# Attention with a mixture of experts: expert 0's first 384 rows are turned by TensorE instead of DMA transposes, and the planner's ranks are set anew

## The chip, the cores and the metric

One core of one Trainium2 chip. The metric is the device time of one execution in microseconds; shown is the median of several runs.

## What is computed

Local attention with a linear position bias over 8 batches, 8 heads, 576 positions and head size 64, then a layer of 8 experts in which each of the 4608 rows goes to its two best by noisy logits:

```python
mask = (rel >= 0) & (rel < 128)
scores = np.where(mask, q @ k.T / 8 - slope * abs(rel), -1e9)
x = (softmax(scores) @ v).reshape(4608, 512)
noisy = x @ w_gate + log1p(exp(x @ w_noise)) * noise
top2 = the two largest of the 8 noisy logits of a row, weighted by softmax
for e in range(8):
    h = np.maximum(x[mask] @ w1[e], 0.0)           # 512 -> 1024
    out[mask] += weight[mask] * (h @ w2[e])        # 1024 -> 512
```

## The kernel before

**Stages.** The attention goes through 32 pairs of heads: scores into banks of the accumulator memory (L557, L568), bias and row maximum on VectorE (L572), exponentials on ScalarE (L596), transposes of the weights by TensorE (L610, L614), copies out (L306 or L310, the two branches of one helper), masks on GpSimd (L633, L634), the product with the values (L647, L656). Per batch the result `xu` is turned into rows (L816), scaled and stored to DRAM (`xs`); a small product gives the gate logits (L849), and `route` makes from them, on all engines, the list of rows of each expert (`slots`, L1039).

**Expert 0 starts early.** Its first 1024 rows are three blocks, `first[0]` to `first[2]`: 384 rows known after batch 4, 384 after batch 6, 256 after batch 7 (`FIRST`, L28). The rest of expert 0 (192 rows) and the other experts' wide blocks of 512 rows, which save multiplications by sums of quarters (L1521), come after the attention.

**A block's way.** `first_ids` loads the row numbers; `tokens` (L1364) gathers 128 rows at a time by an indirect DMA from GpSimd's queue (L1369) into one of three buffers; `turn_tokens` (L1470) calls `fit` (L1444): ScalarE sums squares (L1463), VectorE makes powers of two (L536 to L1455), ScalarE or VectorE writes the high fp16 part (L1465), VectorE the low part (L1466). The two parts are then turned by two DMA transposes issued on SP's queue, in `across` (L1484, L1487), into `xhe` and `xle`, features on partitions. The parts' buffers (`partr`, three pairs) come free only when both have landed (L1480, L1481), and the block is ready when all its tiles are.

**The products.** Each matrix is split in an fp16 high and low part. A first product of a step (`mm1`, L1492) is 12 instructions (4 chunks of features by 3 combinations of parts), `middle` makes the two parts of the hidden rows, and a second product (`mm2`, L1641) adds 3 instructions for each 128 rows; a block has 8 steps of 128 hidden columns. The weights of a step are loaded through small buffers (`raw`, L1353) and split (L1358, L1359). Banks: until the attention's scores are all done, the scores hold four; then three go to the ring `yb` of the second product and one to the ring `hbr` of the first; the attention's other banks join `hbr` when it ends (`banks`, L1778).

**The order.** All instructions are issued in a fixed order for each engine, written out when the program is built. A small planner (`Order`, L110) runs the strands as coroutines with estimated durations and takes, on each engine, the ready operation of the lowest rank; `either` lets ScalarE or VectorE take a copy, whichever comes first. The ranks are sums of a place in the work and tuned constants (`GATE`, `ROUTE`, `FINE`, `STAGE` and so on, L44 to L70). An engine runs its list strictly in that order. In `route`, batches in `QUICK` do seven small elementwise operations (L910 to L912 and L980 to L983) on VectorE, the others on GpSimd.

```python
ring_ = partr if blk in first else tpr
yield either(0.61, 0.6, FINE[108] + rank, LATE[6], lambda e: copy(e, hi[0:r], xg[0:r, 0:DM], scale=up_))
for src, to in ((hi, blk.xh), (lo, blk.xl)):
    spawn(across(src[0:r], to[:, :, cs], rank, landed))
```

Of the kernel before, what the change touches and what calls it, by code (L numbers as in the profile page):

```python
# [9 lines left out]
F16 = mybir.dt.float16  # L10
# [4 lines left out]
OP = mybir.AluOpType  # L15
# [25 lines left out]
WIDE, HALF = 512, 256  # L41
REST = CAP - 2 * WIDE
BLOCKS = tuple(((FROWS, c - FROWS),) if z < NF else ((0, WIDE), (WIDE, WIDE), (2 * WIDE, c - 2 * WIDE)) for z, c in enumerate(CAPS))
ZERO, EMPTY = -382.3, -19  # L44
LOAD = 2072.8
VALUES = -625.0
GATE = (3971.6, 412.2, 111.3, 51.8, 791.7, 789.6, 2069.7, 1294.1)
ROUTE = (335.8, 1160.5, 1403.3, 167.8, 383.8, 836.8, 2175.7, 1956.5)
SCATTER = (-4836.6, 2231.2, -4386.9, -2680.6, 1116.4, -5442.0, 1062.3, 4922.0)
FFN0, FFN1 = -16.7, 677.3  # L50
WEIGHTS = (4140.0, 489.6)
TOKENS = -1020.1
FINE = (-127.3, 1947.0, 7173.5, 490.3, -2780.2, 5954.0, 637.9, -361.7, -649.3, -210.9, -151.3, -905.5, -37.6, -1880.9, 2484.8, 98.4, -658.3, 297.3, -173.4, 348.7, 1057.7, 92.6, 695.5, -338.5, 101.0, 1053.3, -1871.9, 74.4, -170.0, -319.0, 74.0, -244.9, -243.9, 2608.1, 50.9, -18.3, 1061.6, 362.2, -2980.7, 6.3, -2268.2, -402.2, 2094.6, -340.9, 153.2, 699.4, 5518.7, -1010.4, -3064.5, 46.0, -483.1, -595.9, 36.8, -151.2, -384.2, -24.7, 993.6, 28.1, -542.3, -548.0, -4777.1, -2371.4, -0.2, -3348.7, -476.4, -550.6, -2493.0, -1125.3, -1392.5, -827.5, -398.3, -1585.4, -5878.8, 2224.6, 938.3, 3072.0, 4384.7, -465.1, 1415.1, 15.0, -1827.3, -4500.0, 1363.2, -386.3, 3864.4, 4822.7, 160.2, 214.5, 46.3, -2198.5, 357.9, 461.9, -49.1, 263.5, -4035.4, 145.2, -2994.6, 13.2, -185.1, -304.8, -311.6, -535.4, -382.4, 47.0, -739.9, -1144.9, 1496.2, 256.4, 138.3, 640.0, 1746.2, 227.4, 1127.5, -4604.4, -1176.0, -5921.3, -64.4, -1108.1, -841.1, -109.7, -946.5, -120.2, -801.1, -639.7, 262.5, -2170.2, -215.4, 592.8, 436.1, 508.3, 558.9, 299.5, 3603.8, 608.9, 607.1, -370.9, -4584.9, -169.7, -701.5, -4103.9, 1089.3, 315.2, -1365.3, -2191.1, 3868.8, -73.9, -531.1, 7.5, 949.6, 1615.7, -226.8, 149.6)
STAGE = (1189.0, -287.5, 1897.0, -16.5, 17.2, 982.3, 1489.3, 922.7)
MIDDLE = 1219.1
RESULT = 718.4
SIZES = (1329.5, 5070.7, 6603.9)
SOON = -530.0
TIGHT = (1, 5, 7)
QUICK = (5,)  # L60
LATE = (1469.7, 178.7, 538.9, 1188.3, 2256.5, -632.2, -940.3, -218.8, 1749.2, -1178.9, -1654.2, -1776.8, -2806.5, -183.7, -5853.3)
LAG = 0.2
ADD, TWS = 0.34, 5
BEHIND = 176.2
TURN, MARGIN, LATE_BY = (0.3, 0.3), 1.0, 1.0
TURNED = 7e4
SLACK = 0.8
PACE, READ_BY, AHEAD = 1.1, 2.0, 268.0
HELD = 3
SWITCH, NEAR = 0.093, 447.5  # L70
TOP, SOFT, SPLIT = (1.25, 1.25, 0.76), (1.56, 1.56, 0.8), (0.85, 1.35, 0.85)
SP_COST = 0.45
DMA_RATE = 300e3
# [36 lines left out]
class Order:  # L110
# [16 lines left out]
    def spawn(self, strand):  # L127
        self.alive += 1
        self.at(self.now, lambda: self.advance(strand, None))
# [31 lines left out]
    def put(self, ring, tile_):  # L161
        ring.free.append(tile_)
        self.serve(ring)
# [105 lines left out]
def attention_moe(ctx: ExitStack, tc: tile.TileContext, qk_, v, w_gate, w_noise, noise, w1, w2,  # L269
                  out, xs, slots, eye):  # L270
    nc = tc.nc
    ctx.enter_context(tc.manual_schedule())
    main = ExitStack()
    const = ctx.enter_context(tc.tile_pool(name="const", bufs=1))
# [9 lines left out]
    spawn, put, mark = order.spawn, order.put, order.set  # L284
# [4 lines left out]
    def pe(us, rank, emit, join=True, mode="full"):  # L289
        return Op((("PE", us, rank),), emit, join, mode)  # L290
# [4 lines left out]
    def dve(us, rank, emit, join=True, port=False):  # L295
        return Op((("DVE", us, rank),), emit, join, None, port)
# [4 lines left out]
    def either(a, b, rank, late, emit):  # L301
        return Op((("ACT", a, rank), ("DVE", b, rank + late)), emit)

    def copy(e, o, i, **kw):
        if e == "ACT":
            nc.scalar.activation(o, i, AF.Copy, **kw)  # L306
        elif kw:
            nc.vector.tensor_scalar(o, i, kw["scale"], None, op0=OP.mult)  # L308
        else:
            nc.vector.tensor_copy(o, i)  # L310
# [20 lines left out]
    n = len(units)  # L331
# [9 lines left out]
    rel, rel4 = scratch[0][:, 0:W], scratch[0][:, W:2 * W]  # L341
    rel5 = scratch[1][:, 0:BW]
    ident = const.tile([128, 128], F32, name="ident")
    bias = const.tile([128, H, BW], BF16, name="bias")
    bias4 = const.tile([128, NP, W], BF16, name="bias4")
    own_key = const.tile([128, 64], F32, name="own_key")
# [37 lines left out]
    def masks():  # L384
        def folded():
            usual = rel5[:, 64:192]
            nc.vector.tensor_scalar(own_key, rel4[:, 0:64], 0.0, None, op0=OP.is_ge)
            nc.vector.tensor_scalar(usual, rel4, 0.0, float(W), op0=OP.is_lt, op1=OP.mult)
            nc.vector.tensor_add(usual, usual, rel4)
            nc.vector.tensor_copy(rel5[:, 0:64], usual[:, 64:128])  # L390

        def of_first():
            first_ = rel5[:, 192:320]
            nc.vector.tensor_copy(first_[64:128], rel5[64:128, 64:192])
            nc.vector.tensor_scalar(first_[0:64], rel4[0:64], 0.0, 2.0 ** 40, op0=OP.is_lt, op1=OP.mult)
            nc.vector.tensor_add(first_[0:64], first_[0:64], rel4[0:64])

        def bias_of(e, h):
            copy(e, bias[:, h], rel5, scale=slope(h))
            part = slice(h // 2 % 2 * 64, h // 2 % 2 * 64 + 64)  # L400
            copy(e, bias4[part, h // 4 * 2 + h % 2], rel5[part, 64:192], scale=slope(h))

        yield dve(0.14, FINE[0] + -40, lambda: nc.vector.tensor_scalar(ident, rel, 0.0, None, op0=OP.is_equal))
        yield dve(0.14, FINE[1] + -40, lambda: nc.vector.tensor_scalar(before, rel, 0.0, None, op0=OP.is_lt))
        yield dve(0.7, FINE[2] + -40, folded)
        yield dve(0.7, FINE[3] + -40, of_first)
        for g in range(NP):
            for h in (2 * g, 2 * g + 1):
                yield either(0.65, 0.45, FINE[4] + -20 + 5 * g, LATE[9], lambda e, h=h: bias_of(e, h))
            mark(biased[g])  # L410
# [70 lines left out]
    hbr, yb = Ring([]), Ring([])  # L481
# [7 lines left out]
    def loads():  # L489

        for k in range(PAIRS):
            rank = 5 * k - LOAD
            t = qks[k] = yield (qkr, FINE[5] + rank)
            left[k] = len(GROUPS)
# [6 lines left out]
    def all_values():  # L501
        for y in range(2 * B):
            rank = 10 * y - VALUES
            if y == 0:
# [167 lines left out]
    def unit(u):  # L672
        k, gr = units[u]
        blocks = GROUPS[gr]
        t = k * NQ + blocks[0]
        r0, r1, r2, r3, r4, r5, r6, r7 = (t + z for z in STAGE)
        last = gr == 2
# [97 lines left out]
    def rows(b, last, t):  # L775
# [3 lines left out]
        nr, nz = 64 if last else 128, len(blocks)  # L779
        rank = t - GATE[b]  # L780

# [25 lines left out]
    def row_major(b, i, xu, den, t, done):  # L807

        rank = t - GATE[b]
        rows = 64 if i == 4 else 128  # L810
# [27 lines left out]
    def gate(b, blocks, xu, den, t, done):  # L838


        rank = t - GATE[b]
        nz, i = len(blocks), blocks[0]
# [52 lines left out]
    def route(b):  # L895
# [4 lines left out]
        ln, pl = lp[:, 0], lp[:, 1]  # L900
        rank = 20 * b - ROUTE[b]
        V = nc.vector
# [138 lines left out]

        rank = 20 * b + SCATTER[b]
        yield (listing, FINE[63] + rank)
# [106 lines left out]
    first = [Block(0, s0, c, cut * S, own) for (s0, c, cut), own in zip(FIRST, rings1)]  # L1150
# [9 lines left out]
    def weight_rank(e, f):  # L1160

        return 1000 + step_of(e) + f - 4 if e else WEIGHTS[0] + WEIGHTS[1] * f

# [119 lines left out]
    def early_sizes():  # L1283

        yield biased[NP - 1]
        for e in range(EARLY):
# [7 lines left out]
            yield done  # L1294
            yield from powers_of_weights(e, SIZES[e])

# [173 lines left out]
    def turn_tokens(blk, j, r, xg, rank):  # L1470
        yield max(order.now + 3.4, order.transfer(order.now, 2048.0 * r))
        hi, lo, ring_, got = yield from fit(blk, j, r, xg, rank)
        put(xgr if blk in first else xpr, xg)
        mark(blk.weighed)
        yield order.now + MARGIN
        landed = Event(2)
        cs = slice(j * 128, j * 128 + r)
        for src, to in ((hi, blk.xh), (lo, blk.xl)):
            spawn(across(src[0:r], to[:, :, cs], rank, landed))
        yield landed  # L1480
        put(ring_, got)  # L1481
        mark(blk.ready)

    def across(src, to, rank, landed, size=TURNED):  # L1484

# [288 lines left out]
    def first_tokens():  # L1774
        for z, blk in enumerate(first):
            yield from tokens(blk, ranks1[8 * z] - TOKENS)

# [206 lines left out]
    with ExitStack() as ob:  # L1984
# [3 lines left out]
        with tc.For_i(0, reach, 1) as j:  # L1988
            e = nc.values_load(tab[:, 0, bass.ds(j, 1)], engines=[mybir.EngineType.SP], min_val=0, max_val=E - 1)
            r = nc.values_load(tab[:, 1, bass.ds(j, 1)], engines=[mybir.EngineType.SP], min_val=0,  # L1990
                               max_val=(E * EROWS - 128) // LESS)
# [13 lines left out]
            t = op.tile([128, 4, 128], F32, name="ot")  # L2005
# [18 lines left out]
            o = ow.tile([128, DM], F32, name="oo")  # L2024
# [44 lines left out]
```

## Time and profile before

| | |
|---|---|
| median of 3 runs | 979.95 us (979.79 to 980.11) |
| the profiled execution's own time | 978.81 us |
| its span, first to last instruction | 977.1 us |
| mean granted TensorE clock | 0.99 |
| TensorE busy | 943.9 us (97%) |
| VectorE busy | 802.2 us (82%) |
| ScalarE busy | 583.7 us (60%) |
| GpSimd busy | 365.0 us (37%) |
| DMA transposes of `xhe` and `xle` over the whole run | 22 and 22 |

Times in the trace count from the first instruction. PE is TensorE's matrix products, PEld its weight loads, DVE VectorE, ACT ScalarE, POOL GpSimd, SPq the DMA queue of SyncE. The granted clock is the share of TensorE's full speed: 1.00 is 2.4 GHz, 0.50 is 1.2 GHz, and a value between is a mean over a stretch. The drawn length of one product includes its latency, so that products in a row overlap: their rate is seen from their starts. The share of busy time is a mean over stages with different limits: up to about 220 us the attention, from there the experts.

### The profile page before, as it was taken

Reading aid. Unit: us, or ns where it says so; the run is one execution under the profiler, and the core shown is the slowest. Engines: PE = TensorE matmul, PEld = TensorE weight load, DVE = VectorE, ACT = ScalarE, POOL = GpSimd, SP = SyncE. Lnnn points to the kernel's source line nnn. Section 1 sums busy time; section 2 is a strip of 40 time slices with the busy share of each in tenths; the row PEclk is TensorE's granted clock in tenths of the full one; section 3 lists DMA queues with packets and bytes.
Section 4 is the critical chain, followed back from the end, with each engine's and each line's share of the span. In section 5 each row is a group of like instructions: output and inputs, shape, how many; then the busy total and the mean of one; then the engine's idle time right before and its main releaser. Section 6 shows DMA issues by size and latency. Waiting matters only on the chain. (4 is left out here: it accounts for less than half of the span.)

```text
span 977.1 us, 25069 instructions
## 1 busy us (share of the span) xinstructions
PE 943.9 (97%) x8896; PEld 663.7 (68%) x8896; DVE 802.2 (82%) x2768; ACT 583.7 (60%) x1554; POOL 365.0 (37%) x577
## 2 busy tenths in 40 slices
PE   7999999869999999999999999999999999999996
PEld 5777777645557857786677768675867586667753
DVE  8989999979568979997979898978878798979520
ACT  8999988754455745666545556654656365546312
POOL 4467676774424033321342323233322412241113
PEclk9999999989999999999999999999999999999998
DMA  9688998777799797997978889958996969876123
GB/s 330 230 301 273 285 339 271 225 186 148 176 244 180 221 209 148 182 238 201 172 142 202 199 145 210 246 133 161 164 269 140 230 157 235 133 178 127 21 33 52
DMA packets 237151, 188.87 MB, mean 193 GB/s; under 512 B 147872, under 2 KB 191168, under 8 KB 237024
## 3 DMA queue, kind: packets, MB, share of 16 engines
q1 hardware_dynamic: 219680, 148.31, 59.5%
q0 software_dynamic: 17344, 38.94, 21.4%
q8 instruction: 70, 1.15, 0.5%
q14 instruction: 57, 0.47, 0.2%
HBM read 116.24 MB, written 40.71 MB: 161 GB/s over the span
## 5 line engine op out<-in xcount | busy, mean ns | idle before, releaser
L1756 POOL DMA_INDIRECT out_dram<-yo,ix x69 | 116.4, 1687 | 248.2 <-ACT yo L306 142.9
L1652 PEld LDWEIGHTS <-hh 128*128 128x128 f16 x896 | 87.5, 98 | 86.3
L1620 ACT ACTIVATE hh<-bank 128x256 f16<-128x256 f32 (+8 forms) x131 | 45.7, 353 | 114.8 <-PE bank L1521 63.8
L1369 POOL DMA_INDIRECT xp<-xs_dram,ix x35 | 39.8, 1136 | 190.9 <-DVE ix L1116 98.3
L1652 PE MATMUL bank<-w2ha,hh 128*128 128x512 f16 x288 | 109.2, 379 | 0.0
L1652 PE MATMUL bank<-w2la,hh 128*128 128x512 f16 x288 | 109.2, 379 | 0.0
L1652 PE MATMUL bank<-w2ha,hl 128*128 128x512 f16 x288 | 109.2, 379 | 0.0
L596 ACT ACTIVATE p<-p,nm 128x128 f32<-128x128 f32 x256 | 99.1, 396 | 4.2 <-DVE nm L572 4.1
L1521 PEld LDWEIGHTS <-wth 128*128 128x128 f16 x896 | 87.3, 98 | 15.5
L1620 ACT ACTIVATE hh<-c 128x256 f16<-128x256 f32 (+1 forms) x100 | 50.8, 525 | 58.6 <-DVE c L1590 58.2
L306 ACT ACTIVATE yo<-bank,gw 128x512 f32<-128x512 f32 (+6 forms) x61 | 41.7, 686 | 70.3 <-PE bank L1652 45.3
L1652 PEld LDWEIGHTS <-hl 128*128 128x128 f16 x448 | 43.9, 98 | 52.8
L572 DVE CUSTOM_DVE_ANT_0 p<-bank,bias 128x128 f32<-128x128 f32 x288 | 67.0, 285 | 0.3
L306 ACT ACTIVATE c<-bank 128x256 f32<-128x256 f32 x98 | 36.8, 380 | 48.9 <-PE bank L1521 46.8
L557 PE MATMUL bank<-qk 64*64 64x192 f32 (+2 forms) x1152 | 59.2, 325 | 6.8 <-DMA qk<-in_qk_dram 4.6
L1581 DVE TENSOR_TENSOR c<-bank,c 128x512 f32<-128x512 f32 x56 | 38.5, 687 | 30.9 <-PE bank L1521 30.0
L647 PE MATMUL bank<-pT,vraw 128*64 128x128 f32 (+1 forms) x640 | 58.8, 332 | 3.7 <-POOL pT L634 2.5
L1521 PE MATMUL bank<-xhe,wth 128*128 128x256 f16 x224 | 61.1, 273 | 0.0
L1521 PE MATMUL bank<-xlw,wth 128*128 128x256 f16 x224 | 61.1, 273 | 0.0
L1521 PE MATMUL bank<-xhw,wtl 128*128 128x256 f16 x224 | 61.1, 273 | 0.0
L1521 PE MATMUL bank<-xhw,wth 128*128 128x256 f16 x224 | 61.1, 273 | 0.0
L1521 PE MATMUL bank<-xhe,wtl 128*128 128x256 f16 x224 | 61.1, 273 | 0.0
(338 smaller groups left out, 3079.5 us busy)
## 6 DMA issues: line engine op xcount, KB each, us to landing
raw<-in_w_dram SPq DMA_DIRECT2D x144, 256.0 KB, 4.6
mraw<-in_w_dram SPq DMA_DIRECT2D x56, 512.0 KB, 6.1
qk<-in_qk_dram SPq DMA_DIRECT2D x32, 576.0 KB, 5.6
vraw<-in_v_dram SPq DMA_DIRECT2D x16, 640.0 KB, 6.7
out_dram<-xg SPq DMA_DIRECT2D x20, 512.0 KB, 6.4
xs_dram<-x SPq DMA_DIRECT2D x72, 128.0 KB, 4.2
out_dram<-yo,ix POOLq DMA_INDIRECT x69, 5.7
xs_dram<-xg SPq DMA_DIRECT2D x2, 512.0 KB
```

What stands on the lines that cost most here:

```text
L306: nc.scalar.activation(o, i, AF.Copy, **kw)
L557: nc.tensor.matmul(s[h][r * 64:r * 64 + 64, o:o + n_ * 64], qk[half, m * 64:m * 64 + 64], blocks_of(qk[half, QW:QW + S], first_, step, n_) ...
L572: nc.vector.tensor_tensor_reduce(out=o, in0=i, in1=by, scale=-0.125, scalar=3.0e38, op0=OP.add, op1=OP.min, accum_out=m)
L596: nc.scalar.activation(pv, pv, AF.Exp, bias=nm[:, z, h:h + 1], scale=-1.0, accum_out=den[:, i, 2 * g + h:2 * g + h + 1])
L647: nc.tensor.matmul(y, t[:, kb, hh:hh + D], w, start=m == 0, stop=m == len(lst) - 1)
L1369: nc.gpsimd.indirect_dma_start(out=o, out_offset=None, in_=xs[0:blk.rows], in_offset=bass.IndirectOffsetOnAxis(ap=blk.at[0:r, j:j + 1], ax ...
L1521: nc.tensor.matmul(t, wp[:, at + kc], xp[:, 2 * o + kc], start=not add and kc + z == 0, stop=kc + z == 3, skip_group_check=add)
L1581: yield dve(0.6, FINE[125] + rank - MIDDLE, lambda: nc.vector.tensor_tensor(both, y, both, op=OP.add))
L1620: nc.scalar.activation(o, i, AF.Relu)
L1652: nc.tensor.matmul(blk.y[j], h[:, cs], wp, start=a == 0 and z + m == 0, stop=a == 3 and z + m == 3)
L1756: ins = nc.gpsimd.indirect_dma_start(out=out, out_offset=bass.IndirectOffsetOnAxis(ap=blk.ix[0:r, j:j + 1], axis=0), in_=t[0:r], in_offset ...
```

## The change

For the first block alone, the two parts of each 128 rows are no longer sent through DMA transposes. A bank of the second product's ring is taken, seen as fp16 (2 parts x 4 chunks x 128 columns), eight TensorE transposes per 128 rows write into it (24 in all), and two copies of 128x512 by ScalarE or VectorE bring the turned parts to `xhe` and `xle` (six in all). The parts' buffers come free after the copies. An fp16 identity is made at the start. Batch 6 joins `QUICK`. All of the planner's rank constants have new values, so that the order may differ anywhere; the durations that the planner assumes are the old ones.

```diff
-QUICK = (5,)
+QUICK = (5, 6)
-STAGE = (1189.0, -287.5, 1897.0, -16.5, 17.2, 982.3, 1489.3, 922.7)
+STAGE = (1235.4, -299.1, 2758.5, 66.9, 68.8, 3072.9, 2531.1, 1334.1)
-TOKENS = -1020.1
+TOKENS = -1033.3
-FFN0, FFN1 = -16.7, 677.3
+FFN0, FFN1 = -16.4, 567.8
...
+    ident16 = const.tile([128, 128], F16, name="ident16")
...
+        yield dve(0.14, FINE[152] + -40, lambda: nc.vector.tensor_scalar(ident16, rel, 0.0, None, op0=OP.is_equal))
...
         mark(blk.weighed)
+        if blk is first[0]:
+            yield from turned_here(blk, j, r, hi, lo, rank)
+            put(ring_, got)
+            return
         yield order.now + MARGIN
...
+    def turned_here(blk, j, r, hi, lo, rank):
+
+        a = yield (yb, FINE[153] + rank)
+        t = a.bitcast(F16).rearrange("p (z c n) -> p z c n", z=2, c=4)
+
+        def turn():
+            for z, src in enumerate((hi, lo)):
+                for c in range(4):
+                    nc.tensor.transpose(t[:, z, c, 0:r], src[0:r, c * 128:c * 128 + 128], ident16[0:r, 0:r])
+
+        yield pe(0.45, FINE[154] + rank, turn)
+        cs = slice(j * 128, j * 128 + r)
+        done = Event(2)
+        for z, to in enumerate((blk.xh, blk.xl)):
+            spawn(out_of_turn(to[:, :, cs], t[:, z, :, 0:r], rank, done))
+        yield done
+        put(yb, a)
+        mark(blk.ready)
+
+    def out_of_turn(o, i, rank, done):
+        yield either(0.57, 0.6, FINE[155] + rank, LATE[6], lambda e: copy(e, o, i))
+        mark(done)
```

## Rows read from the trace of the kernel before

**Rows 1.** Busy time by stretches: PE, PEld, DVE, ACT, POOL; clock, DMA share, GB/s.

```profile
20.00:160.00 140.00, 136.55 (x2277) 100.87 (x2277) 133.37 (x807) 131.73 (x560) 89.45 (x209) 1.00 0.88 290
160.00:200.00 40.00, 35.46 (x515) 25.75 (x512) 38.43 (x211) 30.01 (x119) 26.98 (x51) 0.96 0.77 229
200.00:208.00 8.00, 5.43 (x82) 3.93 (x79) 7.73 (x24) 5.19 (x17) 5.59 (x7) 1.00 0.71 191
208.00:222.30 14.30, 8.87 (x70) 5.16 (x69) 7.64 (x39) 3.94 (x11) 9.94 (x20) 0.64 0.73 206
222.30:240.00 17.70, 17.70 (x126) 10.93 (x122) 16.89 (x76) 9.15 (x23) 10.23 (x25) 1.00 0.71 121
240.00:961.20 721.20, 719.50 (x5579) 502.54 (x5578) 581.08 (x1508) 384.58 (x755) 210.53 (x224) 1.00 0.82 174
```

**Rows 2.** TensorE's waits from 160 to 225 us: total, times, longest.

```profile
PE bank L647 <- POOL pT L634: 2.5, 2, 1.8
PE bank L610 <- ACT gt L306: 1.8, 1, 1.8
PE bank L656 <- POOL pTl L634: 1.8, 1, 1.8
```

**Rows 3.** The timeline of TensorE: start, length; in brackets idle before it.

```profile
217.12 1.97 PE L816 MATMUL bank<-ident,xu 128*128 128x128 f32 x8
...
222.28 0.32 PE L1495 MATMUL bank<-xhe,w1ha 128*128 128x384 f16 x1
...
251.03 0.33 PE L1495 MATMUL bank<-xhe,w1ha 128*128 128x384 f16 x1
...
281.52 0.27 PE L1495 MATMUL bank<-xhe,w1ha 128*128 128x256 f16 x1
...
319.60 0.27 PE L1521 MATMUL bank<-xhw,w1hb 128*128 128x256 f16 x1
```

**Rows 4.** The timeline of ScalarE (first line) and VectorE: the first block's fit.

```profile
193.49 0.19 ACT L1463 ACTIVATION_READ_ACCUMULATOR th<-xg 128x1 f32 x1
...
198.35 0.28 DVE L572 CUSTOM_DVE_ANT_0 p<-bank,bias 128x128 f32<-128x128 f32 x1
...
198.56 0.15 DVE L536 TENSOR_SCALAR fit<-fit 128x1 int32<-128x1 int32 x1
...
205.15 0.73 DVE L1466 SCALAR_TENSOR_TENSOR th<-xg,fit,th 128x512 f16<-128x512 f32 x1
```

**Rows 5.** The timeline of SP's DMA queue: start, time the issue held it.

```profile
204.89 1.34 SPq L1487 DMA_TRANSPOSE xhe<-th  x1
...
213.04 1.22 SPq L1487 DMA_TRANSPOSE xle<-th  x1
...
214.31 3.17 SPq L1353 DMA_DIRECT2D raw<-in_w_dram  x6
...
236.45 1.22 SPq L1487 DMA_TRANSPOSE xle<-th  x1
...
263.59 1.29 SPq L1487 DMA_TRANSPOSE xle<-th  x1
...
301.81 1.52 SPq L1487 DMA_TRANSPOSE xlw<-th  x1
```

**Rows 6.** The tile xhe from 200 to 300 us: its transposes' landing.

```profile
DMA to landing us min/median/max: 7.9/7.9/7.9
```

**Rows 7.** The timeline of TensorE: runs of small instructions.

```profile
160.87 0.58 PE L963 MATMUL bank<-hot,hot 128*80 128x64 f16 x10
...
189.65 1.09 PE L816 MATMUL bank<-ident,xu 128*128 128x128 f32 x8
```

**Rows 8.** Groups by line and shape: count | busy us, mean ns | idle.

```profile
L816 PE MATMUL bank<-ident,xu 128*128 128x128 f32 x96 | 15.1, 293 | 0.1
...
L306 ACT ACTIVATE xu<-bank 128x512 f32<-128x512 f32 x16 | 9.5, 593 | 7.9 <-PE bank L647 7.9
```

**Rows 9.** The timeline of VectorE: a wait for batch 6's GpSimd operations.

```profile
217.32 0.44 DVE L918 MAX8 tp<-l 128x8 f32<-128x8 f32 x5 [3.92 <-POOL l L983]
```

More of the change, by code (lines that the diff above doesn't have):

```diff
@@ L43 @@
 BLOCKS = tuple(((FROWS, c - FROWS),) if z < NF else ((0, WIDE), (WIDE, WIDE), (2 * WIDE, c - 2 * WIDE)) for z, c in enumerate(CAPS))
[L44 to L49, printed above, removed]
-FFN0, FFN1 = -16.7, 677.3
-WEIGHTS = (4140.0, 489.6)
-TOKENS = -1020.1
-FINE = (-127.3, 1947.0, 7173.5, 490.3, -2780.2, 5954.0, 637.9, -361.7, -649.3, -210.9, -151.3, -905.5, -37.6, -1880.9, 2484.8, 98.4, -658.3, 297.3, -173.4, 348.7, 1057.7, 92.6, 695.5, -338.5, 101.0, 1053.3, -1871.9, 74.4, -170.0, -319.0, 74.0, -244.9, -243.9, 2608.1, 50.9, -18.3, 1061.6, 362.2, -2980.7, 6.3, -2268.2, -402.2, 2094.6, -340.9, 153.2, 699.4, 5518.7, -1010.4, -3064.5, 46.0, -483.1, -595.9, 36.8, -151.2, -384.2, -24.7, 993.6, 28.1, -542.3, -548.0, -4777.1, -2371.4, -0.2, -3348.7, -476.4, -550.6, -2493.0, -1125.3, -1392.5, -827.5, -398.3, -1585.4, -5878.8, 2224.6, 938.3, 3072.0, 4384.7, -465.1, 1415.1, 15.0, -1827.3, -4500.0, 1363.2, -386.3, 3864.4, 4822.7, 160.2, 214.5, 46.3, -2198.5, 357.9, 461.9, -49.1, 263.5, -4035.4, 145.2, -2994.6, 13.2, -185.1, -304.8, -311.6, -535.4, -382.4, 47.0, -739.9, -1144.9, 1496.2, 256.4, 138.3, 640.0, 1746.2, 227.4, 1127.5, -4604.4, -1176.0, -5921.3, -64.4, -1108.1, -841.1, -109.7, -946.5, -120.2, -801.1, -639.7, 262.5, -2170.2, -215.4, 592.8, 436.1, 508.3, 558.9, 299.5, 3603.8, 608.9, 607.1, -370.9, -4584.9, -169.7, -701.5, -4103.9, 1089.3, 315.2, -1365.3, -2191.1, 3868.8, -73.9, -531.1, 7.5, 949.6, 1615.7, -226.8, 149.6)
@@ L54 @@
-STAGE = (1189.0, -287.5, 1897.0, -16.5, 17.2, 982.3, 1489.3, 922.7)
[L55 to L58, printed above, removed]
+ZERO, EMPTY = -1717.1, -19
+LOAD = 5805.0
+VALUES = -1156.0
+GATE = (3497.0, 552.0, -72.8, 105.8, 607.5, 848.8, 1802.4, 1248.6)
+ROUTE = (1229.1, 1099.1, 2641.1, 425.7, 379.3, 1128.2, 1752.3, 1867.2)
+SCATTER = (-5849.4, 2075.8, -4417.3, -3415.7, -149.1, -5144.8, -2198.5, 8121.8)
+FFN0, FFN1 = -16.4, 567.8
+WEIGHTS = (3494.5, 1230.6)
+TOKENS = -1033.3
@@ new lines @@
+FINE = (1659.9, 1149.0, 3054.3, 1123.7, -4771.6, 10025.6, 1545.6, 142.5, -669.6, -1475.9, 609.1, -725.9, -161.1, -1462.1, 1924.9, 33.9, -1495.9, -1094.0, 2143.2, 1838.5, 668.2, 875.6, 721.0, -907.2, -172.0, 1806.9, -198.1, -221.1, -2297.2, -1373.6, 142.0, 554.3, 1143.0, 2468.9, -276.6, -6.4, 109.9, 407.0, -3316.7, 0.7, -1337.7, -94.3, 1709.1, -374.0, -319.4, 23.2, 6303.5, -1535.1, -3283.8, 332.0, -814.2, -1427.5, 126.9, -99.6, -299.7, -2392.7, -279.2, -17.7, 11.2, -976.5, -7262.7, -2312.9, -12.1, -4434.6, -565.4, 219.2, -3835.6, -815.4, -1307.2, -1018.2, -425.5, -1213.2, -10777.0, 1841.1, 353.4, -2070.6, 5976.4, -467.2, 1840.2, 40.3, -2048.2, -6779.6, 3045.2, 15.6, 6421.6, 6355.1, 2117.1, 181.4, 46.3, 4074.0, 1140.6, 1228.8, -1652.1, -2207.9, -6192.3, -3337.9, -2903.6, -550.1, 982.5, -5544.2, -484.1, -486.7, 831.1, 47.0, -1504.8, 102.2, 2523.6, 752.3, 1435.0, 1097.6, 2769.0, 222.5, 6387.8, -11480.7, -2235.6, -5151.7, -60.2, -6237.0, -543.0, -4496.5, -369.3, -355.8, -670.1, -319.8, 455.1, -1399.6, -987.0, -1747.1, 621.8, 439.9, 657.9, -98.3, 2067.6, 1152.5, -448.9, 0.2, -2359.1, -172.6, -3018.5, -5193.4, 3667.1, 257.3, -2711.9, -1130.1, 4906.5, -77.5, -5006.3, 105.3, -2541.9, -252.3, 228.5, 168.9, 364.9, -2690.6, -111.1, 395.7)
@@ L59 @@
+STAGE = (1235.4, -299.1, 2758.5, 66.9, 68.8, 3072.9, 2531.1, 1334.1)
+MIDDLE = 1210.0
+RESULT = 635.3
+SIZES = (1584.5, 2378.0, 5988.9)
+SOON = -752.4
 TIGHT = (1, 5, 7)
-QUICK = (5,)
-LATE = (1469.7, 178.7, 538.9, 1188.3, 2256.5, -632.2, -940.3, -218.8, 1749.2, -1178.9, -1654.2, -1776.8, -2806.5, -183.7, -5853.3)
+QUICK = (5, 6)
+LATE = (2188.5, -1458.4, 545.1, 1914.9, 2008.6, -486.5, -638.1, -511.3, 1765.1, 1392.8, -2720.8, -1841.9, -4466.4, 3144.6, -8335.8)
 LAG = 0.2
 ADD, TWS = 0.34, 5
-BEHIND = 176.2
+BEHIND = 142.8
@@ L67 @@
 SLACK = 0.8
-PACE, READ_BY, AHEAD = 1.1, 2.0, 268.0
+PACE, READ_BY, AHEAD = 1.1, 2.0, 304.3
 HELD = 3
-SWITCH, NEAR = 0.093, 447.5
+SWITCH, NEAR = 0.093, 410.4
 TOP, SOFT, SPLIT = (1.25, 1.25, 0.76), (1.56, 1.56, 0.8), (0.85, 1.35, 0.85)
```

## The prediction

> **What bounds the kernel now.** I read the busy time by stretches first. From 240 us on TensorE is busy for 719.5 of 721.2 us at a granted clock of 1.00, and from 222.3 to 240 without a gap [rows 1]: there the end can move only if TensorE is given less work or starts it earlier. All that TensorE loses by waiting lies ahead of 222.3, and most densely right before it. From 208 to 222.3 it is busy 8.87 of 14.3 us at a mean granted clock of 0.64, so much of even this busy time ran at the lower of the two levels (1.2 GHz, not 2.4); from 200 to 208 it is idle 2.57 us, from 160 to 200 4.54 us, and in the 140 us before that 3.45 us [rows 1].
>
> The list of TensorE's waits names what it waits for there: masked attention weights from GpSimd and copies from ScalarE [rows 2]. These are the latencies of the last attention batch, with no other work to put between. The other work exists: the three early blocks of expert 0. Their first product starts at 222.28 [rows 3], exactly where the idling stops. So the stretch is bounded by when those 384 rows are ready.
>
> Why are they ready so late? The last of their three square sums ends at 193.68; the powers made from them start only at 198.56, when VectorE has finished the last scores, and the last of the three low parts ends at 205.88 [rows 4]. Then six DMA transposes stand on SP's queue from 204.89 to 214.26, each holding the queue about 1.2 us, with three small loads between [rows 5], and a transpose lands 7.9 us after its issue [rows 6]: 213.04 + 7.9 = 220.9. The weight loads for later steps of this block are queued behind, at 214.31 [rows 5].
>
> **The change, part by part.**
>
> Removed: six DMA transposes. SP gets 6 x 1.2 = 7.4 us back, and the six weight loads behind them can go out when their buffers come free, at best some 7 us earlier. The landing no longer counts: the rows could be ready at 205.9 plus the new path.
>
> Added on TensorE: 24 transposes of 128 fp16 columns with their weight loads. No such instruction is in the trace. The nearest below is the listing product (ten fp16 products of 64 columns in 0.58 us, 0.058 each); the nearest above is the fp32 transpose, whose single duration has a mean of 293 ns, though eight in a row take only 1.09 us because they overlap [rows 7, 8]. So 24 cost between 1.4 us (0.058 each) and 7.0 us (0.293 each). I take 0.08, near the fp16 row and under the 0.136 that the pipelined fp32 ones show: 1.9 us.
>
> The Trainium skill has a rule against the change here: "TensorE: Matmul & The Clock Gate", section "Part 4: PE-mode transpose", gives about 275 ns for one 128x128 transpose of a 2-byte type inside a kernel and says that this mode does not raise the clock. By it the 24 would take an estimated 6.6 us, and the sum below would be a gain of 2.0 in place of 6.7. The trace's eight in 1.09 us disagree with adding up single durations; whether the clock counts transposes no row here isolates.
>
> Added on ScalarE and VectorE: six copies of 128x512 from a bank. ScalarE's copy of that shape from fp32 takes 593 ns [rows 8]; six are 3.6 us. Between 208 and 222.3 VectorE is busy only 7.64 us [rows 1], and ScalarE has gaps too, so I cost all but the last pair at nothing; if VectorE, busy 7.73 of the 8 us before, had to do them all ahead of attention's work, 3.6 us would be the upper bound, and below nothing is excluded since they replace no copy.
>
> Ready time: last low part 205.9, its eight transposes 0.64, its two copies in parallel 0.6, and some 0.8 for four hand-overs: about 208.0 instead of 222.3. The banks used are the second product's. They come from the scores, whose last reader ends at 198.63 [rows 4], and the second product wants them only after a first one; I cost no wait there. One bank only is open to the first product until attention ends, so first and second products of this block must alternate; the block holds enough for that, for its eight steps fill most of the gapless stretch from 222.28 to the second block's first product at 251.03 [rows 3], 28.8 us, against the 8.6 that are wanted.
>
> What that gives: how much work does 208 to 222.3 hold? A clock of 0.64 means that 72% of the stretch was at the half level; of 8.87 busy us 6.4 count half, 2.5 whole: 5.7 us at full clock. The same eight transposes show it directly: 1.97 us from 217.12, 1.09 from 189.65 [rows 3, 7]. Filled with products, the 14.3 us hold 5.7 us of attention and 8.6 us of products that no longer stand after 222.3. **Less 1.9 us for the transposes: 6.7 us.**
>
> Is what comes next in time if everything after 222.3 moves up by 6.7? The second early block's last transpose is issued at 236.45 + 1.22 and lands by 245.6, its first product starts at 251.03: 5.5 us of slack. Its fit waits for parts buffers that the first block holds until its transposes land; freed at about 208 instead of 221, that chain, too, moves up by several us. The third block: issue ends 264.9, lands 272.8, needed at 281.52: 8.7. The first wide block: issue ends 303.3, lands 311.2, needed at 319.60: 8.4 [rows 3, 5, 6]. So 6.7 just fits.
>
> Batch 6's seven small GpSimd operations go to VectorE. VectorE idled 3.92 us for the last of them [rows 9], inside the stretch where it has time; I cost this at nothing, bounded by a gain of about 2 us on that chain and a loss of the same on VectorE. The fp16 identity is one more small operation in the start-up: nothing, hidden behind the first load.
>
> The ranks, set anew, may move anything. Their bounds are from the rows: at best they also close the 4.54 + 2.57 us idle of 160 to 208 (7.1 us) and the 0.8 us that a clock of 0.96 costs there; at worst they lose as much. I take zero.
>
> New waits: the transposes stand in TensorE's queue waiting for VectorE's low parts, and attention's tail is queued behind them; the copies wait for TensorE, and the block's first product for them.
>
> **Sum.** 978.81 us for the profiled execution (span 977.1) less 6.7 is 972.1; the median of the runs shown stands 1.14 above that execution, so 979.95 - 6.7 = 973.25, rounded 973.2.
>
> **Rivals.**
> - *The order closes more.* Powers of these rows waited from 193.7 to 198.6 and later for a crowded VectorE; ranks that bring them forward let products in from about 200. Half of the 7.9 us on top gives 969.2, all of it 965.3. For: the first two batches of losses are of the same kind. Against: VectorE is 96% busy from 160 to 200, 38.43 of 40 us [rows 1], so it comes out of attention.
> - *Transposes don't pipeline.* At 0.293 us each, the mean duration of the fp32 ones, they take 7.0 us and leave a gain of 1.6: 978.35. For: each tile's eight wait for a different low part, so they may not follow one another closely. Against: eight took 1.09 us [rows 7], and TensorE has gaps there to take them. (The rule of the Trainium skill's section "Part 4: PE-mode transpose" would give 977.9 here, by its 275 ns.)
> - *Hidden anyway.* A later step keeps its date: the wide blocks' chain of sizes, weights and transposes, with 8.4 us of slack now, slips by the order of SP's queue and takes the 6.7 us back as one wait near 310. 979.9.
> - *Slower: TensorE stands in its own queue.* If the new order puts the transposes where low parts ought to be soon after the squares (193.7 + about 2.5 = 196) but VectorE delivers at 205.9, TensorE stands up to 9.3 us with attention's tail behind it, then gains the 6.7: 2.6 slower, 982.6. It decides once the standing exceeds 8.7 us. For: the order is static, and VectorE is the crowded engine. Against: before the change the same kind of order left single waits of at most 1.8 us [rows 2].
> - That the change doesn't do what it says: the condition picks the first block plainly; no chance given.
>
> **How the numbers follow.** 0.2% is 2.0 us, about what a measurement here can tell from no change. Forecast (gain of 3.5 to 10, which takes in a second block that comes 1.2 us late, copies in the way, and 1.4 us of transposes) 0.50; more closed 0.22; transposes that don't pipeline 0.08; hidden 0.08; slower 0.12. Faster: the first two, 0.72. Same: 0.16, the next two. Slower: 0.12. The range goes from 965.5, nearly all closed, to 980.5, the hidden case with its spread; the slower case and a little at the bottom stay out.
>
> **What would show it.** Right: first product of expert 0 near 208; 24 transposes spanning about 2 us; six fewer DMA transposes, weight loads up by 5 us or more; granted clock near 1.00 from 208 to 222; the first wide product near 313 without a wait before it. Wrong: a first product still after 215 (weights or powers late), a new wait of TensorE on VectorE's low parts, a gap at the second block's or the wide block's start, or TensorE idle risen in 20 to 200.

## The result, and the profile after

The changed kernel takes 987.5 us (median of its runs, 984.53 to 996.97) beside 980.11 us for the kernel before on the same chip: ratio 1.0084, 95% interval 1.0063 to 1.0105. It is 0.84% slower. The forecast was 973.2 us with a range up to 980.5; it was wrong in sign as well as in size. The profiled execution took 986.91 us, with a span of 985.2 us. Its trace has six fewer DMA transposes of `xhe` and `xle`: 19 and 19 whose source is `th`, against 22 and 22 before (14 and 14 more, from `thw` and `tlw`, are in both).

Busy time by stretches of the changed kernel (PE, PEld, DVE, ACT, POOL; clock, DMA share, GB/s), against [rows 1]:

```profile
160.00:200.00 40.00, 35.82 (x523) 26.26 (x523) 38.24 (x201) 33.65 (x124) 26.92 (x57) 0.96 0.76 238
200.00:208.00 8.00, 6.15 (x100) 4.69 (x100) 7.79 (x43) 7.23 (x29) 6.59 (x14) 1.00 0.90 269
208.00:222.30 14.30, 10.76 (x131) 8.02 (x128) 13.65 (x66) 7.02 (x17) 6.52 (x13) 1.00 0.30 60
340.00:420.00 80.00, 75.92 (x533) 51.22 (x532) 57.86 (x159) 37.36 (x71) 27.99 (x28) 0.98 0.84 179
420.00:969.00 549.00, 545.12 (x4306) 383.21 (x4305) 442.70 (x1133) 299.07 (x581) 156.31 (x164) 1.00 0.76 165
```

Two things are to be seen. In 208 to 222.3 TensorE has more to do and a granted clock of 1.00, but VectorE is now busy 13.65 of 14.3 us, where [rows 1] had 7.64. And where TensorE had been idle for 1.7 us of 721 in all from 240 on [rows 1], it is now idle for 4.08 us from 340 to 420 and 3.88 us from 420 to 969.

The timeline of TensorE, changed kernel (start, length, in brackets idle before), against [rows 3]:

```profile
212.74 0.65 PE L1498 MATMUL bank<-ident,th 128*128 128x128 f16 x8
...
219.00 0.61 PE L1498 MATMUL bank<-ident,th 128*128 128x128 f16 x8
...
221.87 0.33 PE L1524 MATMUL bank<-xhe,w1ha 128*128 128x384 f16 x1
...
318.25 0.27 PE L1550 MATMUL bank<-xhw,w1hb 128*128 128x256 f16 x1
...
412.40 0.24 PE L1524 MATMUL bank<-xh,w1hb 128*128 128x192 f16 x1 [3.53 <-DVE hl L1664]
```

Expert 0's first product starts at 221.87, not at 208: 0.41 us earlier than before. The first wide product is 1.35 us ahead of [rows 3]. The last product of the program stands at 975.87, where the kernel before has 967.87. So the change has gained 1.35 us by 318 and loses over 9 us behind it, the largest single piece in the gap of 3.53 us at 412.40.

**Why no early start.** The timeline of VectorE, changed kernel, against [rows 4]:

```profile
206.48 0.14 DVE L538 TENSOR_SCALAR fit<-fit 128x1 int32<-128x1 int32 x1
...
212.28 0.65 DVE L1468 SCALAR_TENSOR_TENSOR th<-xg,fit,th 128x512 f16<-128x512 f32 x1
...
217.92 0.73 DVE L1468 SCALAR_TENSOR_TENSOR th<-xg,fit,th 128x512 f16<-128x512 f32 x1
```

The square sums end at 195.96, 2.3 us later than before. But the powers start at 206.48 instead of 198.56, and the last low part ends at 218.65 instead of 205.88: the new order puts attention's and the routing's VectorE work ahead of the fit. (Batch 6's seven operations, new on VectorE, take 1.7 us of it.) The transposes shortened a path whose front the new ranks had lengthened by 12.8 us.

**Where the loss is made.** First the list of VectorE's waits, 340 to 969 us, then ScalarE's, then TensorE's from 223 to 976 (total, times, longest), all of the changed kernel:

```profile
DVE yo L308 <- DMA out_dram<-yo,ix: 7.1, 3, 4.7
...
ACT yo L306 <- DMA out_dram<-yo,ix: 2.5, 2, 1.9
...
PE bank L1524 <- DVE hl L1664: 6.7, 5, 3.5
```

The timelines of GpSimd and of VectorE at the largest of them, and from 340 to 969 us the landing times of the scatters, all of the changed kernel:

```profile
401.04 4.59 POOL L1785 DMA_INDIRECT out_dram<-yo,ix  x1 [6.30 <-ACT yo L306]
...
411.33 0.75 DVE L308 TENSOR_SCALAR yo<-bank,gw 128x512 f32<-128x512 f32 x1 [4.68 <-DMA out_dram<-yo,ix]
412.00 0.35 DVE L1664 SCALAR_TENSOR_TENSOR hl<-bank,hh 128x192 f16<-128x192 f32 x1
```

```profile
DMA to landing us min/median/max: 4.3/5.5/10.2
```

Read them together. There are three result buffers, and a wide block has four result copies; the fourth takes the buffer that the first one's scatter has read. That scatter was issued at 401.04 and has the longest landing of all, 10.2 us, so its buffer is free at 411.24: the copy starts at 411.33. Behind the copy, in VectorE's queue, stand the hidden rows (hl) of the next narrow block. They free the banks that TensorE's first product of that block needs, so TensorE stops until 412.40. The planner reckons 2.05 us for a scatter and 4.0 us more until its buffer is free; that covers the median of 5.5, not the tail.

### The profile page after: what moved, and what is told of

It is laid out like the page before. It is cut to its first block, busy times and chain, and to the rows that moved or that the text cites. A ratio compares the mean times of both kernels' runs of the same rounds, so it can differ in the third digit from the quotient of the medians.

```text
span 985.2 us, 25144 instructions
## 1 busy us (share of the span) xinstructions
PE 948.1 (96%) x8920; PEld 665.6 (68%) x8920; DVE 801.9 (81%) x2772; ACT 594.8 (60%) x1564; POOL 367.4 (37%) x570
## 4 chain that ended last, share of the span: by engine, by line
PE 72%; DVE 16%; DMA 7%; issue 3%; ACT 1%; POOL 1%; POOLq 0%; DVEq 0%; ACTq 0%
PE bank L1681 26%; PE bank L1550 23%; PE bank L1524 6%; PE bank L1686 4%; DMA out_dram<-yo,ix 4%; PE bank L1674 3%; DVE p L574 3%; PE bank L649 3%; PE bank L559 2%; DMA xp<-xs_dram,ix 2%; DVE bank L580 1%; DVE x L821 1%; PE bank L818 1%; PE bank L612 1%; DMA qk<-in_qk_dram 1%
## 5 line engine op out<-in xcount | busy, mean ns | idle before, releaser
L1785 POOL DMA_INDIRECT out_dram<-yo,ix x69 | 120.6, 1748 | 253.4 <-ACT yo L306 138.6
L306 ACT ACTIVATE yo<-bank,gw 128x512 f32<-128x512 f32 (+6 forms) x57 | 38.9, 685 | 73.3 <-PE bank L1681 59.9
L1649 ACT ACTIVATE hh<-c 128x512 f16<-128x512 f32 (+1 forms) x98 | 50.0, 524 | 48.2 <-DVE c L1619 29.9
L559 PE MATMUL bank<-qk 64*64 64x192 f32 (+2 forms) x1152 | 61.2, 329 | 6.5 <-DMA qk<-in_qk_dram 4.6
L1327 ACT ACTIVATE mraw<-mraw 128x1024 f32<-128x1024 f32 x56 | 58.7, 1048 | 5.2 <-DMA mraw<-in_w_dram 5.2
L1550 PE MATMUL bank<-xle,wth 128*128 128x256 f16 x224 | 61.1, 273 | 0.0
```

Of the source, the lines that this page charges most:

```text
L559: nc.tensor.matmul(s[h][r * 64:r * 64 + 64, o:o + n_ * 64], qk[half, m * 64:m * 64 + 64], blocks_of(qk[half, QW:QW + S], first_, step, n_) ...
L1327: yield act(us, FINE[82] + rank, lambda: nc.scalar.activation(v, v, sum_, accum_out=o))
L1550: nc.tensor.matmul(t, wp[:, at + kc], xp[:, 2 * o + kc], start=not add and kc + z == 0, stop=kc + z == 3, skip_group_check=add)
L1649: nc.scalar.activation(o, i, AF.Relu)
L1785: ins = nc.gpsimd.indirect_dma_start(out=out, out_offset=bass.IndirectOffsetOnAxis(ap=blk.ix[0:r, j:j + 1], axis=0), in_=t[0:r], in_offset ...
```

## The experiments

The kernel before was timed beside each; its medians there go from 981.25 to 983.02 us, beside 980.11 in the result, so ratios compare better than times.

**Run 1: five result buffers.** The changed kernel with every engine's order of instructions kept; two more buffers in memory that attention has left.

```
-        t = yield (yor, FINE[146] + rank)
+        token = yield (yor, FINE[146] + rank)
+        t = yos.pop(0)
+        yos.append(t)
...
-        put(yor, t)
+        put(yor, token)
...
+        yos.extend(bias.rearrange("p a b -> p (a b)").bitcast(F32)[:, z * DM:z * DM + DM] for z in range(2))
```

> The changed kernel, every engine's order of instructions the same, with five result buffers in turn instead of three, so that a result copy no longer meets the landing of the scatter that read its buffer. Theory A (the loss is made behind 223 us, by result copies that stand on a scatter's landing with the hidden rows of the next narrow block queued behind them): the TensorE gaps of 3.53, 1.2, 0.98, 0.76 and 0.5 us and most of the 1.7 us at the lower clock after the first go, so the time falls by 6 to 8.5 us from 987.5 to 979 to 981.5 us, and no result copy waits over 0.3 us for a scatter. Theory B (the 24 transposes and the six copies, or the traffic in DRAM, are what costs): the gaps stay or move and the time stays at 986 to 988 us.

980.59 us, ratio to before 0.999 (0.9975 to 1.0005). Busy time from 404 to 421 us, first the changed kernel, then this run:

```profile
404.00:421.00 17.00, 13.47 (x144) 13.03 (x142) 9.59 (x37) 6.42 (x13) 6.48 (x8) 0.90 0.76 177
```

```profile
404.00:421.00 17.00, 17.00 (x185) 15.65 (x183) 14.04 (x44) 9.80 (x20) 8.55 (x8) 1.00 0.83 201
```

The hole is gone, and the clock of 0.90 with it. TensorE's wait for hl falls from 6.7 us to 0.2, no result copy waits for a scatter, and the time falls by 6.9 us (987.5 to 980.59), or from 0.84% behind the kernel before to level with it. Theory A holds: this loss is the result copies', not the transposes'. Two waits of another kind remain, 2.43 us at 275.92 and 1.51 us at 809.16.

**Run 2: the same buffers in the kernel before.**

> The kernel before, in its own order, with five result buffers instead of three. Theory A: the kernel before shows one such wait, 1.05 us on ScalarE, and 1.5 us of TensorE gaps in all behind 223 us, so it gains 0 to 1 us: 979 to 980 us. If the third buffer were what limits every version alike (theory B's form of it), it would gain as much as the changed kernel does, 6 us or more.

978.79 us, ratio 0.997 (0.9957 to 0.9984): by the ratio 3 us less, more than the 0 to 1 of theory A and well under the 6 of its rival. The kernel before has one such wait, 1.1 us on ScalarE, and it costs TensorE little. From the list of its TensorE's waits, 223 to 976 us:

```profile
PE bank L1495 <- DVE hl L1635: 1.5, 4, 0.6
```

In run 2 this wait is 0.6 us. Where the rest of the 3 us comes from stays open.

**Runs 3 and 4: half the change each.** Run 3 has the new code and the old ranks and `QUICK`. Run 4 has the new ranks and keeps the DMA transposes:

```
-        if blk is first[0]:
+        if False:
             yield from turned_here(blk, j, r, hi, lo, rank)
```

> The transposes by TensorE alone: the changed code with the ranks of the kernel before. Theory A with its second half (the early start of expert 0 was there to be had, and the new ranks gave it away by setting the fit of the fp16 parts 12.8 us later): low parts end near 206, the first product of block 0 starts at 208 to 211 us, and the time is 972 to 976 us. Theory B (the transposes cost, or the product finds another wait): first product at 216 us or later and 979 to 985 us. A third possibility, that the old ranks do not fit the new code and the result copies stand on scatters here too: first product near 208, but the gain taken back behind 223 us, 978 to 985 us.

> The new ranks alone: the DMA transposes stay. Theory A: the result copies stand on scatters as in the changed kernel, and the low parts are late while the DMA transposes still take their 8 us, so the first product comes at 227 to 236 us, and the time is 988 to 998 us. Theory B (the transposes by TensorE are what costs): 978 to 982 us, as before.

Run 3: 1006.63 us, ratio 1.0245 (1.0217 to 1.0274), slower than either theory has it; first product at 224.33, and the first wide product at 335.65, 16.05 us later than in [rows 3]. Run 4: 1002.06 us, ratio 1.0198, first product at 227.80. Run 4 lies 4 us above theory A's range and excludes theory B. Run 3 tells nothing about the transposes: the separate step that builds the fp16 unit matrix, at time 0, had shifted the order of all that follows. Ranks and code are set for each other, and "undo one half" here measures an order nobody chose.

**Run 5: the transposes alone, in the old order.** Both unit matrices in one step, so that the planner sees nothing new until the low parts:

```
-        yield dve(0.14, FINE[0] + -40, lambda: nc.vector.tensor_scalar(ident, rel, 0.0, None, op0=OP.is_equal))
-        yield dve(0.14, FINE[152] + -40, lambda: nc.vector.tensor_scalar(ident16, rel, 0.0, None, op0=OP.is_equal))
+        yield dve(0.14, FINE[0] + -40, unit_matrices)
```

**Run 6: the same with five result buffers**, as in run 1.

> The transposes by TensorE with the ranks and QUICK of the kernel before, and the second unit matrix built inside the first one's step, so that every engine's order is that of the kernel before up to the low parts of block 0 (in the earlier run with old ranks, one more step at 0 us had changed the order of everything behind it). Theory A: the low parts end near 206 us, the first product starts at 208 to 211 us, TensorE is busy for 11 to 12.5 us of 208 to 222.3 (8 in the kernel before), so 3 to 4 us more work is done by 222.3, less 2 us of transposes that are new; the end comes 2 to 6 us earlier than before, 974 to 979 us, unless result copies stand on scatters behind 223. Theory B (something else, a weight or a bank, holds the first product): first product at 216 us or later, and 979 to 984 us.

> The same order of instructions, with five result buffers in turn instead of three. Theory A: whatever waits for scatters the run before shows behind 223 us go, and the time is that of the early start alone: 973 to 977 us, faster than both kernels. Theory B: no faster than the kernel before with five buffers (978.8 us in the earlier call), 978 to 983 us.

Run 5: first product at 210.85, 988.33 us, ratio 1.0044 (1.0017 to 1.0072). Run 6: first product at 208.52, 989.31 us, ratio 1.0053 (1.0022 to 1.0084). Both times lie outside the ranges of both theories. The early start was there to be had, but it makes nothing faster, and here it isn't the result buffers: run 5 has waits of this kind, 3.2 us in all (0.3 on VectorE, 2.9 on ScalarE), run 6 has none and is no faster. Run 6 by stretches, its TensorE timeline, and its SP queue:

```profile
208.00:222.30 14.30, 13.06 (x121) 8.18 (x116) 13.08 (x52) 8.66 (x21) 10.39 (x19) 1.00 0.80 251
...
300.00:340.00 40.00, 34.91 (x305) 27.88 (x303) 30.81 (x77) 22.02 (x39) 8.36 (x10) 0.91 1.15 200
```

```profile
206.63 1.07 PE L1502 MATMUL bank<-ident,th 128*128 128x128 f16 x16
...
208.52 0.33 PE L1528 MATMUL bank<-xhe,w1ha 128*128 128x384 f16 x1
...
317.04 0.27 PE L1554 MATMUL bank<-xhw,w1hb 128*128 128x256 f16 x1 [2.14 <-DMA xhw<-th]
318.85 0.28 PE L1554 MATMUL bank<-xlw,w1hb 128*128 128x256 f16 x1 [1.53 <-DMA xlw<-th]
```

```profile
297.82 4.61 SPq L1520 DMA_TRANSPOSE xlw<-tlw  x1
302.51 4.77 SPq L1520 DMA_TRANSPOSE xhw<-th  x1
...
314.45 3.65 SPq L1520 DMA_TRANSPOSE xlw<-th  x1
```

At full clock 13.06 us of work are done in 208 to 222.3, where 8.87 at a clock of 0.64 came to 5.7 [rows 1]: 7.4 us more. The transposes are not among them, since eight start at 204.42, the other sixteen at 206.63, and all have ended by 207.7. The second block's first product comes at 243.76, 7.3 us ahead of [rows 3], and 5.6 us of lead are still there when the rest of expert 0 starts (303.11; 308.71 in the kernel before). Then TensorE reaches the first wide block and stands for its DMA transposes: they hold SP's queue for up to 4.8 us each, and the last is issued at 314.45 instead of 301.81 [rows 5]. 5.0 us are waits on xhw and xlw, and the stretch runs at a clock of 0.91.

**Run 7: the first wide block's eight transposes as plain copies, in run 6; run 8: the same in run 2.** Both leave out the turning of that block.

```
-        end = yield Op((("SP", 0.2 + TURN[0] * chunks_, rank),), lambda: nc.sync.dma_start_transpose(to, src))
+        end = yield Op((("SP", 0.2 + TURN[0] * chunks_, rank),), lambda: nc.sync.dma_start(to, src.rearrange("p (c n) -> p c n", n=128)) if plain else nc.sync.dma_start_transpose(to, src))
```

> The run with the old order and five result buffers, but the eight DMA transposes of the first wide block are plain DMA copies of the same bytes in the same places of SP's queue, so that block's fp16 parts are not turned (its rows of the output are left wrong). Theory C (the early start is given back where the first wide product waits for the landing of those transposes, 5.0 us of gaps and 1.7 to 2.4 us at the lower clock in 316 to 330): the gaps on xhw and xlw go, the first wide product starts at 311 to 314 us without a pause, and the time falls by 6 to 8 us, from 989 to 981 to 983 us, with less spread between runs. Theory D (the 316 us stall only shows work that is late anyway, and the rest of the loss lies behind 340): the time falls by less than 3 us.

> The control: the kernel before with five result buffers, with the same eight transposes as plain copies (the first wide block's parts not turned). There TensorE shows no gap at the first wide product, so by theory C nothing changes: 978 to 980 us. If the copies by themselves relieve the DMA engines for other work, this one gets faster too, by 3 us or more, and the run above has to be read against it.

Run 7: 979.15 us, ratio 0.9968 (0.9955 to 0.9981), 10.2 us less than run 6 (by the ratios 0.85%, 8.3 us); run 8: 979.44 us, ratio 0.9971, beside 978.79 and 0.997 in run 2, no change. Run 7, 300 to 340 us:

```profile
300.00:340.00 40.00, 39.46 (x360) 32.37 (x361) 38.66 (x94) 26.94 (x50) 11.22 (x12) 1.00 0.94 221
```

Theory C holds, with more than its price of 6 to 8 us: the early start was being given back at the transposes of the first wide block. The date that it gave was missed: the first wide product starts at 316.36, not at 311 to 314. What is left in run 7 is that it only draws level with run 2. Its first wide product is 4.3 us ahead of run 2's (316.36 against 320.62), its last product 1.0 us behind (968.50 against 967.52). Of these 5.2 us its list of TensorE's waits has 4.3 in short ones, 0.8 at most, for hl and c; run 2's has 0.6.

**Runs 9 and 10: a version meant to beat both.** Run 6's order up to 240 us, five buffers, and new ranks for what follows, in run 9 with five buffers known to the planner, in run 10 with three.

> A version meant to beat both: TensorE's transposes, the old order up to 240 us, five result buffers that the planner knows of, and new ranks for what comes after, chosen so that by the planner's own reckoning the short waits of TensorE for the narrow blocks' hidden rows (0.4 to 0.8 us each, 3.5 us in all in the run with copied transposes) go. The first wide block is turned by DMA as in the kernel before. Theory C: if the first wide block's transposes are still late, TensorE stands on xhw and xlw near 316 us for up to 5 us and the time stays at 980 to 986 us; if the new order sends them out in time, 972 to 977 us. A third outcome, 977 to 980 us, would be that the early start is worth no more than its transposes cost.

> The same, but the planner reckons with three result buffers while five are used in turn. As the run before: 972 to 977 us if the first wide block's transposes land in time, 980 to 986 us if they do not; 1 to 2 us behind the run before, since the planner's reckoning has it so.

Run 9: 977.92 us, ratio 0.997 (0.9945 to 0.9994). Run 10: 985.75 us, ratio 1.0039 (1.002 to 1.0059). Run 9 is the expectation's third outcome. In it the short waits are gone, and 2.6 us on xlw remain; its single times spread from 972.16 to 987.33. Run 10 is in the range given for transposes that land late, and in its trace they do: TensorE waits 10.3 us on xhw and xlw. But that trace is of its longest execution, 993.42 us.

**Runs 11 and 12: keep the row gathers out of the transposes.** GpSimd reads one element of the first wide block's low parts before it issues the second wide block's four gathers; run 12 reads element 7 in place of 13, so that two transposes, not four, hold them back.

```
-                    yield pool(1.25, FINE[92] + rank, lambda: gather(q + 2 * i, 128, xp[:, i * XW:i * XW + XW]))
+                    def gathered():
+                        if blk is second[2] and not q and not i:
+                            nc.gpsimd.tensor_copy(pad, second[1].x[1][0:1, 13, 127:128])
+                        gather(q + 2 * i, 128, xp[:, i * XW:i * XW + XW])
+
+                    yield pool(1.25, FINE[92] + rank, gathered)
```

> The version meant to beat both, with one GpSimd copy of one element more: ahead of the four row gathers of the second wide block it reads the first wide block's low parts of the first row pair, so those gathers (266 KB each, issued at 293 to 300 us in the run before) go out only when four of the eight transposes have landed. Theory E (the gathers, issued in the middle of the transposes, are what stretches these from 1.2 us to 3 to 6 us of SP's queue each): the transposes take 1.2 to 2.5 us each, the last is issued by 306 us, TensorE's gaps on xlw at 318 to 320 (2.6 us) go, and the time falls by 3 to 5 us, to 973 to 975 us, with less spread. Theory F (the transposes are slow for another reason, such as the scatters at 286 to 291 us, or their own number of small packets): the transposes take as long as before, and the time stays at 977 to 980 us.

> As the run before, but GpSimd's element is read from the low parts of the first two of the eight transposes, so the four gathers go out some 4 us earlier, near 299 us. There ScalarE stood 3.73 us for the landing of a gather, with the hidden rows of expert 0's last block queued behind it, and TensorE lost 2.93 us at 313.5. Theory E with this new wait as the only remaining price: that wait falls below 0.5 us, the later transposes still take under 2.5 us each, no TensorE gap over 1 us is left behind 223 us, and the time is 973 to 975.5 us. Theory F: moving the gathers forward again stretches the transposes, TensorE waits on xhw or xlw again for 1 to 3 us, and the time is 976 to 978 us.

The timeline of SP's queue in run 9, then in run 11; the timelines of GpSimd and ScalarE in run 11, and its list of TensorE's waits:

```profile
298.42 5.83 SPq L1519 DMA_TRANSPOSE xlw<-tlw  x1
304.35 4.00 SPq L1519 DMA_TRANSPOSE xhw<-th  x1
```

```profile
298.91 1.25 SPq L1524 DMA_TRANSPOSE xlw<-tlw  x1
300.25 1.78 SPq L1524 DMA_TRANSPOSE xhw<-th  x1
...
304.85 1.24 SPq L1524 DMA_TRANSPOSE xlw<-th  x1
```

```profile
303.40 0.18 POOL L1385 CAST pad<-xlw 1x1 f32<-1x1 f16 x1 [9.00 <-DMA xlw<-tlw]
...
311.71 1.06 ACT L1429 ACTIVATE thw<-xp 128x1024 f16<-128x1024 f32 x1 [3.73 <-DMA xp<-xs_dram,ix]
```

```profile
PE bank L1532 <- DVE hl L1672: 2.9, 1, 2.9
```

Run 11: 977.38 us, ratio 0.995 (0.9927 to 0.9972). The transposes do what theory E says: with the gathers held back the last five take 1.2 to 1.8 us again, and no wait on xlw is left. The time doesn't: it is 0.5 us under run 9's, which the intervals do not tell apart, and lies in theory F's range. The same pattern returns elsewhere: ScalarE's square of a gathered row stands 3.73 us on that gather's landing, the hidden rows of expert 0's last block are queued behind it, and TensorE loses 2.9 us. Run 12: 977.65 us, ratio 0.9959 (0.9946 to 0.9971). TensorE's wait for hl falls to 0.6 us and none on the wide block's transposes comes, but the third early block's transposes now cost 1.6 us at 277.61 and the size of a weight block 1.5 us at 298.96; its first wide product starts at 319.14. So of theory E's signs the gaps and the time fail. In both runs a wait that goes makes room for another between 270 and 320 us.

Run 12 also shows that gathers alone do not stretch a transpose. The timelines of SP's queue and of GpSimd in run 12:

```profile
301.80 1.26 SPq L1524 DMA_TRANSPOSE xlw<-th  x1
...
301.96 1.03 POOL L1374 DMA_INDIRECT xp<-xs_dram,ix  x1 [0.59 <-DVE hh L1659]
```

Its four gathers go out from 301.96 to 306.09, and the three transposes issued beside them take 1.26 to 1.33 us. Holding the gathers back also held back the two scatters behind them in GpSimd's queue (from 305.84 in run 9 to 309.81 in run 11 and 307.75 in run 12). That the gathers are the cause, as theory E has it, is therefore not shown.

Runs 2, 9, 11 and 12 beat both kernels; run 11 has the lowest ratio, half a per cent under the kernel before. But the intervals of 9, 11 and 12 overlap with that of run 2, which has the DMA transposes and no early start: that the early start is worth anything beyond the five buffers is not shown.

## Why the prediction was wrong

- **What bounds the stretch before 222.3: right.** Run 6 fills the hole with products, at a granted clock of 1.00.
- **24 transposes at 0.08 us: right.** Eight take 0.61 to 0.66 us, 1.9 in all, though a single one lasts 220 ns. The Trainium skill's "TensorE: Matmul & The Clock Gate", section "Part 4: PE-mode transpose", has about 275 ns for one; the trace has 220 ns, and eight in a row overlap, so the rival built on adding up single durations falls.
- **Copies: right but for a detail.** 0.59 to 0.60 us each; the last pair ran one after the other on ScalarE, 219.64 to 220.73, not in parallel: 0.5 us late.
- **"Ready time: last low part 205.9": the first step that failed.** It took a date from the old order for a kernel whose ranks are all new. The low part ended at 218.65. In the old order the product starts at 208.52 in run 6, as worked out, and from 209.39 to 211.21 in the other traces of that order; so the path was sized to within 0.5 to 3.2 us and its beginning was not.
- **The sum of 6.7 us: right as a term.** In run 6 the lead is 7.3 us at the second block's first product and 5.6 us at 303.
- **"A transpose lands 7.9 us after its issue": misread, without harm.** The 7.9 us is the landing of one transpose of the third block, issued at 256.80; the trace has no landing of the first block's six. For the first wide block's eight it has one, 11.7 us for the transpose issued at 299.66. That is 311.4, beside the 311.2 of the prediction, which is luck.
- **"So 6.7 just fits": the second step that failed.** At the second and third block it holds in run 6. The slack of 8.4 us at the first wide block was worked out with the queue's traffic of before. In run 6 that block's last transpose was issued 12.6 us later, and TensorE stood on it; run 7 prices this at 8.3 to 10.2 us. In the changed kernel itself it doesn't show, since its products aren't early.
- **"The ranks ... I take zero", with bounds of 7.9 us from the idle of 160 to 208: the third step that failed, and the one that decided the sign.** The loss was made behind 340, in a stretch that I had read as safe since TensorE was never idle there. There result copies stand on scatters that land late, and TensorE waits 6.7 us for the hidden rows queued behind them. Run 1 gives 6.9 us back without touching the order.
- **The rivals.** The slower one, TensorE standing for late low parts, did not happen: TensorE's idle time ahead of the transposes is 0.2 us. (Its own standing, 205.9 less 196, is 9.9 and not 9.3 us.) "Hidden anyway", one wait near 310 that takes the gain back, is what runs 5 and 6 show; there each transpose held SP's queue for longer.

Batch 6's move to VectorE was not tried by itself. What stretches the transposes stays open: in run 11 two of the first took 3.11 and 3.34 us, from 292 to 299, with the gathers held back.

## What to carry to other kernels

A gain in a statically ordered kernel must be followed to the end of the program: ask at every later hand-over what stands at the head of each in-order queue, what it waits for, and who is queued behind it. A stretch in which the critical engine never idles may still have no margin; look at the tail of the landing times, not at the median, wherever a ring of buffers turns on a DMA. And when ranks or priorities change together with code, don't take any date of the old trace for the new one: state the early date as a condition, with a price for missing it.

## What was not expected of the hardware

- A DMA transpose of 128 rows by 1024 or 768 fp16 elements holds SP's queue for 1.23 us at best (kernel before, at 287.62), but for 2.9 to 5.8 us in run 9 from 294 to 311, and for 1.2 to 1.8 us in run 11 from 299 on. A plain copy in the same place was held as long once (run 7, 5.61 us at 292.36). GpSimd's gathers beside a transpose do not suffice for it (run 12). The Trainium skill's "DMA: Bandwidth & Descriptors", section "SWDGE vs HWDGE vs iDMA", has each DMA engine take turns between the queues that GpSimd's DMAs feed and those that SP's feed; no run here shows that.
- A scatter's landing spreads from 4.3 to 10.2 us around a median of 5.5 in one execution (changed kernel, 340 to 969 us).
- This one is the planner's and not the chip's: one step more in its list at time 0 (run 3 against run 5) is worth 18.3 us through the order it sets, 1006.63 against 988.33 us.
